# Spectral layer and MLP on one core: transform steps at the end of a tick, a first stage over 128 partitions, two tables at other addresses

## The chip, the core and the metric

One core of a Trainium2 chip runs the whole program. The metric is the device time of one launch in microseconds (us), median of three runs. Engines: PE multiplies matrices, PEld is its weight load, ACT (ScalarE), DVE (VectorE) and POOL (GpSimd) work element by element, SP only issues DMAs. PE writes PSUM; ACT and DVE read it; POOL does not.

## The reference

`x` is 4 batches of 3008 x 256 floats. Per batch: a real FFT along the 3008 positions, a complex 256 x 256 product with bias, a soft threshold, the inverse FFT; then an MLP over all 12032 tokens.

```python
X = np.fft.rfft(x, axis=1)
Yr = Xr @ w_r - Xi @ w_i + b_r
Yi = Xr @ w_i + Xi @ w_r + b_i
Yr = np.sign(Yr) * np.maximum(np.abs(Yr) - 0.01, 0.0)      # Yi likewise
y = np.fft.irfft(Yr + 1j * Yi, n=3008, axis=1)
h = y.reshape(12032, 256) @ w_in                            # 256 -> 2048
out = (h / (1 + np.exp(-h))) @ w_out                        # 2048 -> 256
```

## The kernel before

**The transform** is split as 3008 = 47 x 64 and done with tables of sines and cosines as matrix products. The first stage (47 points) goes to DRAM scratch `scr1`; second stage, complex product, threshold and third stage run over 12 steps `u` per batch (2 of 24 residues each) and go to `scr2`; the last stage `i2` reads `scr2` and leaves 512 tokens at a time in `xt`, in the MLP's layout. Precision is kept by splitting each operand in a high and a low part (`fp32r`) and adding three products.

**The MLP** goes in *ticks*: one tick is one block of 512 tokens and 128 of the 2048 hidden channels. `mlp1` (L631, 12 matmuls) writes one of two PSUM banks tagged `h`; ACT applies Silu (L638) and casts the high part `gh` (L647), DVE forms the low part `gl` (L648); `mlp2` (L789, 12 matmuls) adds into the `acc` banks. The `gh`, `gl` of tick t are made at the head of tick t+1 and are used by `mlp2` in tick t+2.

**The order.** `manual_schedule` means that each engine works in the order in which the code issues. A dictionary `fill` holds the transform's work by tick: what is put at an integer t stands between `mlp1` and `mlp2` of that tick, what is put at t + 0.5 stands behind `mlp2`, at the tick's end. A planner fills ticks 24 to 146 for batches 1 to 3 with three kinds of work:

- a *piece* (`stack_split`, `stack_product`, L294 to L317): one sixteenth of the first stage of batch 2 or 3. The 47 rows stand at partitions 0 to 46, and their low parts at 64 to 110, so one product over 111 partitions does both. Its four matmuls (L308) write two banks, which ACT (L312) and DVE (L313) read;
- a *step* (`u3_step` with half 0): the second stage `s2_3` (L417, 8 passes) into one bank, read by ACT L425, L426 and DVE L429; then the split of an earlier threshold result (ACT L474, DVE L475), and the third stage `i1` (L489, 6 matmuls) into another bank, read by ACT L493. A step also issues the loads `a`, `t2` (SP) and `t3` (POOL);
- a *mix* (`u3_step` with half 1): `mix3`, 18 matmuls (L442) into two banks. The first is copied by ACT L448, POOL adds the biases (L449, L450); the second is read by four DVE instructions (L461) of `shrink`, which is deferred to the head of the next tick, ahead of its `gl`.

All of these share two PSUM banks, `d0` and `d1`, one after the other (`bank`, L182). A piece that follows a step therefore writes the bank that `s2_3` wrote and then the bank that `i1` wrote; a piece that follows a mix writes the mix's two banks in turn. Each must wait until the readers are done.

`shift(pool, n)` allocates n bytes that nobody uses, to move what follows it in SBUF. Later there are *fast* ticks (blocks 10 to 22, L717), in which only `i2` is left of the transform.

Of the kernel before, what the change touches and what calls it, by code (L numbers as in the profile page):

```python
# [18 lines left out]
S, D, DFF, NB = 3008, 256, 2048, 4  # L19
RR, KK = 47, 64  # L20
# [129 lines left out]
def spectral_mlp_kernel(ctx: ExitStack, tc: tile.TileContext, x, w_r, w_i, b_r, b_i, w_in, w_out, c1, c2, c3, c4, c3f, c5, out):  # L150
    nc = tc.nc
    cst = ctx.enter_context(tc.tile_pool(name="cst", bufs=1))
    sb = ctx.enter_context(tc.tile_pool(name="sb", bufs=2))
    tf = tc.alloc_tile_pool(name="tf", bufs=1)
# [3 lines left out]
    def shift(pool, n):  # L158

        state["shifts"] += 1  # L160
        pool.tile([128, n // 4], F32, bufs=1, name=f"shift{state['shifts']}")
# [20 lines left out]
    def bank(name):  # L182

        state["d"] += 1
        tag, bufs = f"d{state['d'] % 2}", 1
        if state["prologue"]:
            k = state["d"] % 8
            tag, bufs = (("d0", 1), ("acc", 3), ("h", 2), ("acc", 3), ("d1", 1), ("acc", 3), ("h", 2), ("e0", 1))[k]
        if state["fast"]:
            tag = "d1"  # L190
        return ps.tile([128, 512], F32, tag=tag, bufs=bufs, name=name)
# [3 lines left out]
    def store(dst, src, late=False):  # L195

        if late or not state["prologue"]:
            stores.append((dst, src))
        else:
            nc.scalar.dma_start(out=dst, in_=src)  # L200

    def flush(n):
        for dst, src in stores[:n]:
            nc.sync.dma_start(out=dst, in_=src)
        del stores[:n]
# [17 lines left out]
    def x_load_twice(b, q):  # L223

        t = x_sb[q % 2]
        if b == STACKED and q < 2:
            nc.gpsimd.memset(t[32:64, :], 0.0)
        h, g = divmod(q, 8)
        v = x[b].rearrange("(n h j) d -> n h (j d)", h=2, j=NJ)[:, h, g * 4 * D:(g + 1) * 4 * D]
        for p in (0, 64):  # L230
            nc.gpsimd.dma_start(out=t[p:p + RR, :], in_=v)
        return t
# [3 lines left out]
    def x_ahead():  # L236
        if x_next:
            q = x_next.pop(0)
            x_t[q] = (x_load_twice if q[0] >= STACKED else x_load)(*q)
# [8 lines left out]
    def s1(b, g, late=False):  # L248
        for _ in s1_halves(b, g, late):
            pass  # L250
# [43 lines left out]
    def stack_split(b, q):  # L294
        t = x_t[b, q]
        sx = tf.tile([128, 4 * D], F32R, tag="sx", bufs=1, name="sx")
        nc.scalar.copy(sx[:64 + RR, :], t[:64 + RR, :])
        nc.vector.tensor_sub(sx[64:64 + RR, :], t[64:64 + RR, :], sx[64:64 + RR, :])
        x_t[b, q] = sx

    def stack_product(b, q):
        sx = x_t.pop((b, q))
        o = tf.tile([128, 4 * D], F32, tag="s1o", bufs=2, name="s1o")[:2 * NR, :]
        for i in range(2):
            p = bank("s1")
            c = slice(i * 512, (i + 1) * 512)
            for k in range(2):
                nc.tensor.matmul(  # L308
                    out=p[:, k * D:(k + 1) * D], lhsT=c5_sb[:64 + RR, :],
                    rhs=sx[:64 + RR, (2 * i + k) * D:(2 * i + k + 1) * D], start=True, stop=True,  # L310
                )
            nc.scalar.copy(o[:, c], p[64:64 + 2 * NR, :])  # L312
            nc.vector.tensor_tensor(out=o[:, c], in0=p[:2 * NR, :], in1=o[:, c], op=ALU.add)  # L313
        h, g = divmod(q, 8)
        v = scr1[b].rearrange("r (i h j) d -> (r i) h (j d)", i=2, h=2)
        store(v[:, h, g * 4 * D:(g + 1) * 4 * D], o)
        x_ahead()  # L317
# [15 lines left out]
    def t2_load(b, u):  # L333
        t2 = tf.tile([128, 256], F32, tag="t2", bufs=3, name="t2")
        nc.sync.dma_start(out=t2, in_=c2[:, u * 256:(u + 1) * 256])
        t2_t[b, u] = t2
# [141 lines left out]
    def i1(b, u):  # L478
        z = u_t.pop((b, u))
        t3 = t3_t.pop((b, u))  # L480
        p = bank("i1")
        pv = p.rearrange("p (a c) -> p a c", a=2)
        for r in range(2):
            q = slice(r * 128, (r + 1) * 128)
            if b == 0:
                nc.tensor.matmul(out=pv[:, r, :], lhsT=t3[:, q], rhs=z[:, r, :], start=True, stop=True)  # L486
                continue
            for n, (m, k) in enumerate(((0, 0), (0, 1), (1, 0))):
                nc.tensor.matmul(  # L489
                    out=pv[:, r, :], lhsT=t3[:, m, q], rhs=z[k][:, r, :], start=(n == 0), stop=(n == 2),  # L490
                )
        o = tf.tile([128, 2, D], F32, tag="i1o", bufs=2, name="i1o")
        nc.scalar.copy(o, pv)  # L493
        store(scr2[b][2 * u:2 * u + 2].rearrange("r p d -> p r d"), o)
# [331 lines left out]
    def w_split(t, dst, eng):  # L826
        nc.scalar.copy(dst[0], t)
        eng.tensor_sub(dst[1], t, dst[0])
# [43 lines left out]
    with tc.manual_schedule():  # L872
# [6 lines left out]
        c5_sb = tf.tile([128, 128], F32R, name="c5_sb")  # L879
# [35 lines left out]
        def w_ahead():  # L915
            if weights:
                src, *rest = weights.pop(0)
                w_loaded.append((w64_load(src), *rest))
# [3 lines left out]
        def w_begin():  # L922

            w_ahead()
            if w_loaded:
                w_run.append([0, w64_split(*w_loaded.pop(0))])
                next(w_run[-1][1])
# [27 lines left out]
        def u_step(u):  # L955
            if u < NU:
                if u + 3 < NU:
                    u_load(0, u + 3)
                t3_load(0, u)
                s2(0, u)  # L960
            if u > 2:
                w_go()
            if 0 <= u - 1 < NU:
                mix(0, u - 1)
            if u % 2 and 2 < u < NU:
                w_go()
            if 0 <= u - 2 < NU:
                i1(0, u - 2)

        t2_load(0, 0)  # L970
        for g in range(8):
            s1(0, g)
            if g < 3:
                x_ahead()
# [8 lines left out]
        warm(zero, 5)  # L983
        w_split(w32[0], wr, nc.vector)
        w_split(w32[1], wi, nc.gpsimd)
        for u in range(NU):
            u_step(u)
            if u == 0:
                w_ahead()
            if u == 2:  # L990
                w_begin()
            if u in (3, 4):
                flush(1)
            if u in (2, 3, 5, 7, 9):
                x_ahead()
            if u == 8:
                nc.sync.dma_start(out=c4_sb, in_=c4)
# [16 lines left out]
        g_load(0, 1, cols=slice(2 * D, 4 * D))  # L1014
        s1(1, 4, late=True)
        w_go()
        shift(tf, 192)
        w_tags[:] = [(("zl", 2), ("zh", 2))]
        s1(1, 5, late=True)
        flush(2)  # L1020
# [17 lines left out]
        def at(t, fn, *args):  # L1038
            fill.setdefault(t, []).append((fn, args))
# [33 lines left out]
        steps = []  # L1073
# [12 lines left out]
        done, t, since = 37, 24, 0  # L1086
        while steps or turned:
            boundary = t % NFF == 1 and t > 32
            stage = None
            if not boundary and t not in taken:  # L1090
                b = steps[0][0] if steps else NB
                ready = b in stacked and t >= stacked[b] + (4 if b > 1 else 0)
                apart = 2 + (ready and b > 1 and len(pieces_left) % 2)
                if pieces_left and t >= done + apart and pieces_left[0][0] <= b + 1:
                    stage = "piece"
                elif ready:
                    stage = "mix" if steps[0][2] else "step"
            more = None
            if turned and t >= turned[0][0] and t >= since + 2 and not (boundary and t < turned[0][1]):
                if stage in ("mix", None) or t >= turned[0][1]:  # L1100
                    more = turned.pop(0)[2]
                    since = t
            if stage == "piece":
                at(max(t - 2, done), stack_split, *pieces_left[0])
                at(t, stack_product, *pieces_left[0])
                done = t
                if pieces_left.pop(0)[1] == 15:
                    stacked[max(stacked) + 1] = t
            elif stage:
                if b not in begun:  # L1110
                    begun.add(b)
                    for k in range(2):
                        at(t - 2 + k, u_load, b, k)
                at(t, u3_step, *steps.pop(0))
                last = t
                ended[b] = t
            if more:
                at(t + 0.5 * (stage is not None), *more)
                if more[0] is i2_ends:
                    at(t - 2, i2_load, more[1], True)  # L1120
            t += 1
# [3 lines left out]
        for i in range(FAST[0], len(BLOCKS)):  # L1125
            if i in FAST:
                first = max(16 * i - 13, last + 1)
                t = last_stage(i, first)
# [14 lines left out]
        for q in range(NFF // 2):  # L1143
            steps = fast_weights(q)
# [20 lines left out]
        for t in range(len(ticks) + 1):  # L1165
            i, f = ticks[t] if t < len(ticks) else (LAST, None)
# [68 lines left out]
```

## Time and profile before

| | |
|---|---|
| median of three runs | 1302.69 us (1302.64 to 1303.19) |
| the profiled execution | 1301.09 us |
| its span, first to last instruction | 1298.7 us |
| PE busy in the span | 1285.1 us, 99% |
| ACT, DVE, POOL busy | 790.6, 890.1, 200.3 us |
| TensorE clock granted | 0.998 of full speed |

PE is busy all but 13.6 us of the span, and 92% of the chain that ended last is PE. The matmuls overlap, so that their durations (some 277 ns each) say little; the distance from one start to the next is what a matmul costs, and the chain of waits gives it for a group in one number (1.36 us for 12 matmuls, for example).

### The profile page before, as it was taken

The page shows a single profiled execution, that of the slowest core. Times are in us where ns is not written, and L with a number is a line of the kernel's source. Part 1 is how long each engine was busy: PE and PEld are TensorE (multiplying, and loading weights), DVE is VectorE, ACT ScalarE, POOL GpSimd, SP SyncE. Part 2 cuts the span into 40 slices and gives each one's busy share as a digit, 9 for nine tenths or more (in the row PEclk, how much of TensorE's full clock was granted, in tenths as well). Part 3 has the DMA queues.
Part 4 walks back from the last instruction along what each step waited for, and adds up shares of the span by engine and source line. Part 5 has one row for each costly group of instructions (what it writes and reads, how often), then busy time and mean ns, then how long its engine had stood idle before and what let it go on. Part 6 is the DMA issues. An engine that isn't in the chain of part 4 may idle for free.

```text
span 1298.7 us, 27507 instructions
## 1 busy us (share of the span) xinstructions
PE 1285.1 (99%) x10933; PEld 1259.9 (97%) x10933; DVE 890.1 (69%) x1697; ACT 790.6 (61%) x1640; POOL 200.3 (15%) x296
## 2 busy tenths in 40 slices
PE   8999999999999999999999999999999999999998
PEld 3988999999999999999999999999999999999998
DVE  3777757778767777566658666667666666766663
ACT  5456655767666656555555666566656665666655
POOL 2000002222212221111202111210112101110200
PEclk9999999999999999999999999999999999999999
DMA  8886414554465543423220110011001110110000
GB/s 267 265 239 197 140 52 121 132 150 108 118 161 153 119 130 102 129 82 119 84 75 2 48 33 12 22 33 32 14 11 48 33 32 2 33 33 14 5 24 25
DMA packets 76166, 110.29 MB, mean 85 GB/s; under 512 B 8880, under 2 KB 54824, under 8 KB 76040
## 3 DMA queue, kind: packets, MB, share of 16 engines
q1 hardware_dynamic: 61921, 79.17, 20.8%
q0 software_dynamic: 10544, 25.68, 8.0%
q10 hardware_dynamic: 3575, 3.70, 0.9%
q8 instruction: 86, 1.41, 0.5%
q14 instruction: 40, 0.33, 0.1%
HBM read 71.03 MB, written 37.49 MB: 84 GB/s over the span
## 4 chain that ended last, share of the span: by engine, by line
PE 92%; DMA 4%; ACT 2%; DVE 1%; issue 0%; POOL 0%; SPq 0%; ACTq 0%; DVEq 0%
PE acc L789 38%; PE h L717 19%; PE h L631 16%; PE mix L442 5%; PE s L417 3%; PE i L489 2%; PE mix L382 2%; PE i L558 2%; PE i2e L558 1%; PE s L308 1%; DMA scr<-s1o 1%; PE s L269 1%; DMA t3f<-in_c3f_dram 1%; PE s L351 1%; PE i L486 1%; DMA out_dram<-o 1%
## 5 line engine op out<-in xcount | busy, mean ns | idle before, releaser
L789 PE MATMUL acc<-wout,gh 128*128 128x256 f32 x3008 | 541.4, 277 | 0.0
L789 PEld LDWEIGHTS acc<-wout,gh 128*128 128x128 f32 x3008 | 454.6, 188 | 1.1 <-issue 0.5
L789 PE MATMUL acc<-wout,gl 128*128 128x256 f32 x1504 | 416.3, 277 | 1.4 <-DVE gl L648 1.4
L789 PEld LDWEIGHTS acc<-wout,gl 128*128 128x128 f32 x1504 | 282.3, 188 | 1.8 <-DVE gl L648 1.8
L631 PE MATMUL h<-xt,win 128*128 128x256 f32 x2016 | 259.6, 277 | 0.4 <-ACT xt L590 0.3
L631 PEld LDWEIGHTS h<-xt,win 128*128 128x128 f32 x2016 | 242.6, 188 | 0.8 <-ACT xt L590 0.5
L638 ACT ACTIVATE g<-h 128x512 f32<-128x512 f32 (+1 forms) x177 | 101.9, 576 | 148.2 <-PE h L631 146.6
L765 DVE TENSOR_TENSOR gl<-gp,gh 128x512 fp32r<-128x512 f32 x208 | 145.7, 701 | 25.1 <-ACT gh L764 24.4
L755 ACT ACTIVATE gp<-gp 128x256 f32<-128x256 f32 x104 | 43.5, 418 | 180.1 <-DVE gp L752 180.1
L648 DVE TENSOR_TENSOR gl<-g,gh 128x512 fp32r<-128x512 f32 (+1 forms) x177 | 117.4, 664 | 46.9 <-ACT gh L647 45.4
L764 ACT CAST gh<-gp 128x512 fp32r<-128x512 f32 x208 | 129.5, 622 | 6.5
L647 ACT CAST gh<-g 128x512 fp32r<-128x512 f32 (+1 forms) x177 | 106.2, 600 | 1.1 <-PE acc L789 0.2
L717 PE MATMUL h<-xt,win 128*128 128x256 f32 x624 | 106.2, 279 | 0.0
L757 DVE TENSOR_TENSOR gp<-h,u 128x256 f32<-128x256 f32 x104 | 44.1, 424 | 78.7 <-ACT gp L756 78.7
L461 DVE TENSOR_TENSOR y<-q,mix 64x256 f32<-64x256 f32 x144 | 60.3, 419 | 41.9 <-PE mix L442 35.0
L717 PE MATMUL h<-th,sw_h 128*128 128x256 f32 x312 | 87.4, 280 | 0.0
L717 PEld LDWEIGHTS h<-xt,win 128*128 128x128 f32 x624 | 86.4, 188 | 0.1
L717 PE MATMUL h<-th,sw_l 128*128 128x256 f32 x312 | 86.2, 276 | 0.0
L717 PE MATMUL h<-tl,sw_h 128*128 128x256 f32 x312 | 86.2, 276 | 0.0
L449 POOL TENSOR_TENSOR q<-q,bias 128x256 f32<-128x256 f32 x36 | 28.9, 804 | 340.6 <-ACT q L448 340.6
L752 DVE TENSOR_TENSOR gp<-h,u 128x256 f32<-128x256 f32 x104 | 44.2, 425 | 50.7 <-PE h L717 49.2
L763 ACT ACTIVATE gp<-gp 128x512 f32<-128x512 f32 x104 | 66.3, 638 | 0.0
(169 smaller groups left out, 2325.3 us busy)
## 6 DMA issues: line engine op xcount, KB each, us to landing
a<-scr SPq DMA_DIRECT2D x48, 256.0 KB
x_sb<-in_x_dram POOLq DMA_DIRECT2D x64, 188.0 KB, 3.9
gin<-scr SPq DMA_DIRECT2D x48, 192.0 KB
t<-in_c_dram POOLq DMA_DIRECT2D x36, 256.0 KB, 3.7
scr<-i1o SPq DMA_DIRECT2D x36, 256.0 KB
t<-in_c_dram SPq DMA_DIRECT2D x48, 128.0 KB
scr<-s1o SPq DMA_DIRECT2D x32, 192.0 KB
scr<-s1o SPq DMA_DIRECT2D x13, 384.0 KB
```

What stands on the lines that cost most here:

```text
L442: nc.tensor.matmul(out=out, lhsT=x_[:, e, c, :], rhs=m[:, e, :], start=(n == 0), stop=(n == 5))
L461: nc.vector.tensor_tensor(out=y[64 * i:64 * i + 64, r, :], in0=q[rows, i, :], in1=pv[rows, i, :], op=op,)
L631: nc.tensor.matmul(out=p[:, c:c + D], lhsT=w[:, e, f * 128:(f + 1) * 128], rhs=v[:, e, c:c + D], start=(m == 0), stop=(m == 5),)
L638: nc.scalar.activation(out=g[:, q], in_=p[:, q], func=ACTF.Silu)
L647: nc.scalar.copy(gh[:, q], g[:, q])
L648: nc.vector.tensor_sub(gl[:, q], g[:, q], gh[:, q])
L717: nc.tensor.matmul(out=p, lhsT=w[j], rhs=m[k], start=(begins and n == 0), stop=(n == 2), skip_group_check=True,)
L752: nc.vector.tensor_tensor(out=g[:, 1, :], in0=px[:, 0:HB], in1=u, op=ALU.add)
L763: nc.scalar.activation(out=v, in_=v, func=ACTF.Silu)
L764: nc.scalar.copy(h, v)
L765: nc.vector.tensor_sub(l, v, h)
L789: nc.tensor.matmul(out=a[:, r, :], lhsT=v[:, q], rhs=wout[:, f, w, :], start=(begins and m == 0 and r == 0), stop=(ends and m == 2), skip_ ...
```

## The change

Three edits, all in the transform:

- The piece's product runs over all 128 partitions: ACT casts 128 instead of 111, DVE subtracts on 64 instead of 47, the rows between are set to zero by one more memset on POOL for each of the two buffers.
- Steps and mixes go from t to t + 0.5, behind the tick's `mlp2`. Pieces stay where they are, between `mlp1` and `mlp2`. Work of the last stage (`i2`, `i2_ends`) that shares a tick with a step or a mix goes the other way, from behind `mlp2` to ahead of it.
- Three `shift` calls are added, one gets another size. In the built program the second-stage tables `t2` go from 0 to 192 modulo 256 bytes, the third-stage tables `t3f`, `t3` and the tiles `y`, `i1o` from 0 to 128; `a`, `xh`, `xl` (0) and `zh`, `zl` (192) stay.

In the changed kernel the lines from L228 on are one further (L309 for L308), near the end up to four.

```diff
         if b == STACKED and q < 2:
-            nc.gpsimd.memset(t[32:64, :], 0.0)
+            for p in (32, 96):
+                nc.gpsimd.memset(t[p:p + 32, :], 0.0)
...
-        nc.scalar.copy(sx[:64 + RR, :], t[:64 + RR, :])
-        nc.vector.tensor_sub(sx[64:64 + RR, :], t[64:64 + RR, :], sx[64:64 + RR, :])
+        nc.scalar.copy(sx, t)
+        nc.vector.tensor_sub(sx[64:128, :], t[64:128, :], sx[64:128, :])
...
-                    out=p[:, k * D:(k + 1) * D], lhsT=c5_sb[:64 + RR, :],
-                    rhs=sx[:64 + RR, (2 * i + k) * D:(2 * i + k + 1) * D], start=True, stop=True,
+                    out=p[:, k * D:(k + 1) * D], lhsT=c5_sb,
+                    rhs=sx[:, (2 * i + k) * D:(2 * i + k + 1) * D], start=True, stop=True,
...
+        shift(tf, 192)
         t2_load(0, 0)
+        shift(tf, 64)
...
         w_split(w32[1], wi, nc.gpsimd)
+        shift(tf, 128)
         for u in range(NU):
...
-        shift(tf, 192)
+        shift(tf, 64)
         w_tags[:] = [(("zl", 2), ("zh", 2))]
...
-                at(t, u3_step, *steps.pop(0))
+                at(t + 0.5, u3_step, *steps.pop(0))
...
             if more:
-                at(t + 0.5 * (stage is not None), *more)
+                at(t + 0.5 * (stage == "piece"), *more)
```

PE around a step that a piece follows, before: the `s2_3` rows write the tile `s_3651`, `i1` writes `i_3669`, the piece writes `s_3711` and `s_3716`.

```order
L631 MATMUL h<-xt_2693,win_82 128x256
L417 MATMUL s_3651<-t_3135,a 128x2x64 x4
L489 MATMUL i_3669<-zh,t_2916 128x256
...
L789 MATMUL acc<-wout,gh 128x256 x2
...
L631 MATMUL h<-xt_2692,win_82 128x256
...
L308 MATMUL s_3711<-sx,c_sb 128x256 x2
L308 MATMUL s_3716<-sx,c_sb 128x256 x2
```

The same place after the change, with the tiles under new numbers and the lines one further:

```order
L632 MATMUL h<-xt_2653,win_82 128x256
L790 MATMUL acc<-wout,gh 128x256 x2
...
L418 MATMUL s_3668<-t_3152,a 128x2x64 x4
L490 MATMUL i_3686<-zh,t_2933 128x256
...
L632 MATMUL h<-xt_2652,win_82 128x256
...
L309 MATMUL s_3715<-sx,c_sb 128x256 x2
L309 MATMUL s_3720<-sx,c_sb 128x256 x2
```

Between the end of `i1` and the piece there stood `mlp2` and `mlp1`, 24 matmuls; now there stands `mlp1` alone, 12.

PE from a mix to the piece behind it, before:

```order
L442 MATMUL mix<-ws_80,xl 128x256
L789 MATMUL acc<-wout,gh 128x256 x2
...
L631 MATMUL h<-xt_2692,win_82 128x256
...
L308 MATMUL s_3595<-sx,c_sb 128x256 x2
L308 MATMUL s_3600<-sx,c_sb 128x256 x2
```

And after, where this tick's part of the last stage (L559) has gone ahead of `mlp2`:

```order
L559 MATMUL i_3524<-c_sb,gin 128x141 x2
L790 MATMUL acc<-wout,gh 128x256 x2
...
L443 MATMUL mix<-ws_80,xl 128x256
L632 MATMUL h<-xt_2652,win_82 128x256
...
L309 MATMUL s_3600<-sx,c_sb 128x256 x2
L309 MATMUL s_3605<-sx,c_sb 128x256 x2
```

Here too `mlp2` has gone from behind the mix to ahead of it, and only `mlp1` is left between the mix and the piece.

## Rows read from the trace of the kernel before

**Rows 1.** Page: the span, PE's busy time, the last chain by engine.
```profile
span 1298.7 us, 27507 instructions
PE 1285.1 (99%) x10933; PEld 1259.9 (97%) x10933; DVE 890.1 (69%) x1697; ACT 790.6 (61%) x1640; POOL 200.3 (15%) x296
PE 92%; DMA 4%; ACT 2%; DVE 1%; issue 0%; POOL 0%; SPq 0%; ACTq 0%; DVEq 0%
```
**Rows 2.** Groups by shape, PE: count | busy us, mean ns | idle before.
```profile
L417 PE MATMUL s<-t,a 128*128 128x128 f32 x288 | 38.1, 275 | 0.7 <-DVE s1o L313 0.7
L442 PE MATMUL mix<-wr,xh 128*128 128x256 f32 x144 | 26.3, 276 | 0.0
L308 PE MATMUL s<-sx,c_sb 111*128 111x256 f32 x128 | 20.4, 282 | 0.0
```
**Rows 3.** Timeline of PE, 317 to 335 us: start, duration, what.
```profile
320.59 1.05 PE L417 MATMUL s<-t,a 128*128 128x128 f32 x8
321.39 0.36 PE L489 MATMUL i<-zh,t 128*128 128x256 f32 x1
...
322.19 0.40 PE L789 MATMUL acc<-wout,gh 128*128 128x256 f32 x2
...
324.96 0.64 PE L308 MATMUL s<-sx,c_sb 111*128 111x256 f32 x4
...
330.25 0.39 PE L789 MATMUL acc<-wout,gh 128*128 128x256 f32 x2
```
**Rows 4.** Timeline of ACT, 317 to 335 us.
```profile
321.67 0.59 ACT L425 CAST xh<-s 128x512 fp32r<-128x512 f32 x1 [0.29 <-PE s L417]
322.16 0.38 ACT L426 COPY xs<-s 128x256 f32<-128x256 f32 x1
323.02 0.41 ACT L428 CAST xh<-xs 128x256 fp32r<-128x256 f32 x1 [0.49 <-DVE xs L427]
323.34 0.62 ACT L474 CAST zh<-y 128x512 fp32r<-128x512 f32 x1
323.86 0.58 ACT L493 COPY i1o<-i 128x512 f32<-128x512 f32 x1
...
326.74 1.05 ACT L297 CAST sx<-x_sb 111x1024 fp32r<-111x1024 f32 x1
```
**Rows 5.** Timeline of DVE, 317 to 335 us.
```profile
322.91 0.68 DVE L429 TENSOR_TENSOR xl<-s,xh 128x512 fp32r<-128x512 f32 x1
...
330.52 1.72 DVE L461 TENSOR_TENSOR y<-q,mix 64x256 f32<-64x256 f32 x4 [0.75 <-PE mix L442]
...
333.34 0.69 DVE L648 TENSOR_TENSOR gl<-g,gh 128x512 fp32r<-128x512 f32 x1
```
**Rows 6.** Chain that ended last, 325 to 372 us: start, us, what.
```profile
325.12 0.47 PE s L308 x4
325.59 1.42 PE acc L789 x12
327.01 1.36 PE h L631 x12
...
354.17 1.42 PE h L631 x12
...
369.78 1.41 PE acc L789 x12
```
**Rows 7.** Timeline of PE, 236 to 239 us.
```profile
237.59 1.16 PE L417 MATMUL s<-t,a 128*128 128x128 f32 x8 [0.39 <-DVE s1o L313]
238.50 0.36 PE L489 MATMUL i<-zh,t 128*128 128x256 f32 x1
```
**Rows 8.** Timeline of POOL, 100 to 260 us.
```profile
211.79 0.94 POOL L227 MEMSET x_sb<- 32x1024 f32 x1
...
219.31 0.73 POOL L449 TENSOR_TENSOR q<-q,bias 128x256 f32<-128x256 f32 x1 [4.67 <-ACT q L448]
```
**Rows 9.** Chain that ended last, 715 to 732 us.
```profile
725.02 3.95 DMA gin<-scr
```

## The prediction, made before the changed kernel was run

> **What bounds the kernel now.** I read the page first: PE is busy 1285.1 of 1298.7 us and holds 92% of the last chain [rows 1]. So the end comes later by whatever keeps PE waiting, and earlier by whatever makes its matmuls follow closer. Next the groups by shape: the reader is to see that PE hardly waits for the transform today, 0.7 us in all in front of the second stage (L417), nothing in front of the pieces (L308) or the mixes (L442) [rows 2]. Then the chain, which gives groups of 12 matmuls from start to start: 1.36 us where PE runs evenly, 1.42 us behind a piece and 1.41 us behind a step [rows 6]. Last the timelines of PE, ACT and DVE through one step, one piece and one mix [rows 3 to 5]: they tell how long after PE's last write the two shared PSUM banks are read out.
>
> **Steps at the end of a tick: the term that decides.** A piece must wait for the readers of both banks. The order shows that between a step or a mix and the piece of the next tick one group of 12 goes away: 24 matmuls stood there (2.72 us), now 12 (1.36 us). Counted in the order of the changed kernel, 10 pieces follow directly on a full step, 14 on a mix, 1 on a step that has only the second stage; the other 7 of the 32 follow on neither, or on a third stage alone, whose one copy is short, and I count no wait for them.
>
> *Step, then piece.* The second stage ends at 321.39, where L489 starts, and `i1` at 322.19: 0.80 us [rows 3]. ACT reads the first bank (L425, L426), makes a sum and a split (L428, L474), and only then copies `i1`'s bank: L493 from 323.86 for 0.58, to 324.44, 3.05 us after the second stage [rows 4]. `i1` itself is long done; what is late is ACT's chain, and it starts only when PE delivers, so that an idle ACT doesn't shorten it. After the change PE reaches the piece's second half at 0.80 + 1.36 + 0.24 (half of 0.47 [rows 6]) = 2.40 us. It waits 0.65 us. (The first half needs L429, which ends at 323.59 [rows 5], 2.20 us after; due at 2.16, so this wait lies within the other.) Before, the piece was due 1.36 us later, at 3.76, which is why no wait shows.
>
> *Mix, then piece.* The mix ends at 330.25 [rows 3]. The four L461 that read its second bank run from 330.52 for 1.72, to 332.24, 1.99 us after [rows 5]. PE is there at 1.36 + 0.24 = 1.60: it waits 0.39 us.
>
> *Second stage alone, then piece.* Its only bank is the piece's second; L429's end at 2.20 against 1.60: 0.60 us.
>
> Each wait also costs a restart. One that the trace has in front of a step, at 237.59, shows it: the eight passes of L417 last 1.16 us there and 1.05 without a wait [rows 3, 7], so 0.11. Sum: 10 x 0.76 + 14 x 0.50 + 0.71 = 15.3 us. What queues behind a waiting piece on PE is its tick's `mlp2`, and with it everything: no later slack takes these waits back, since PE has none. The price from below is zero, if the readers were early; from above I add 0.05 per wait for the way from a reader's end to PE, 1.3 in all, an estimate.
>
> *What goes away.* From a piece to the next step or mix there are now 36 matmuls, not 24, so the waits of L417 on DVE L313 go: 0.7 us idle [rows 2] and two restarts, 0.9 us. Nothing else becomes late there: the piece's readers need less than the 2.7 us at which they were just too slow.
>
> *Behind the steps.* `mlp2` no longer follows a step: 36 x 0.05 (1.41 less 1.36) saves 1.8. `mlp1` does now; the row of 354.17, where it follows other transform matmuls, gives 1.42 [rows 6], so up to 36 x 0.06 = 2.2 is paid. I take 0, between -1.8 and 2.2. The 14 parts of the last stage that go ahead of `mlp2` trade one follower for another too: 14 x 0.06 either way, taken as 0.
>
> *DMAs that move.* A step's loads of `a` and `t2` (SP) and `t3` (POOL) leave half a tick later and serve a step at least two ticks on: 0. The stores of `i1` are queued at the end of a tick and leave with the next one. In the order the last `i1` of batch 1 stands five ticks ahead of the part of the last stage that reads it, so one tick less is covered; were it not, each of three batches could pay one load of 3.95 us [rows 9].
>
> **The first stage over 128 partitions.** The four matmuls of a piece take 0.47 us where four of the 128-row kind take 4/12 of 1.36 = 0.45, and their mean is 282 ns beside 276 for L442 of the same size [rows 2, 6]. And `mlp2` behind them takes 1.42, not 1.36. I put both on the 111 rows, as the piece is the one group of this size without 128: 32 x (0.02 + 0.06) = 2.6 us saved. From below 0, if it is something else.
> The Trainium skill speaks against this term: by TensorE: Matmul & The Clock Gate, section LDWEIGHTS (loading the stationary operand), a weight load takes as long over 32 rows as over 128, and only the columns count. By it the 2.6 us would stay, and the sum would be that much higher. The trace rather disagrees, with 282 against 276 ns, but has no matmul at both sizes.
> Around the matmuls: ACT's cast L297 takes 1.05 us [rows 4]; ACT's time goes by columns, not partitions, so 0, and were it by partitions 0.16 more, in ticks where ACT waits for PE anyway (it is busy 61%, [rows 1]). The two more memsets take 0.94 us each on POOL, which idles 4.67 us next to the one shown [rows 8]: 0, at most 1.9 if a load of `x` came late by it.
>
> **The tables' addresses.** No row shows the same matmul at two addresses. The nearest difference of pace between matmuls of one size is 1.42 against 1.36 per 12, 5 ns each; over the 648 matmuls and passes of second and third stage that is 3.2 us either way. I take 0, since nothing says which way.
>
> **Sum.** 15.3 - 0.9 - 2.6 = 11.8 us. The profiled execution took 1301.1 (its span 1298.7 and 2.4 around it): 1312.9. The median of the runs is 1.6 higher, 1302.7, and it is a median that is to be predicted: 1314.5 us. Its own range is 1309 to 1320 by the bounds named.
>
> **Rivals.**
> 1. *The 111 rows cost nothing.* Same waits, no gain from the full rows: 1314.5 + 2.6 = 1317. For it speaks that `mlp2` behind a step is just as slow with 128 rows (1.41); against it that the piece's own four are slow from the first. Chance 0.12. This is what the Trainium skill's page TensorE: Matmul & The Clock Gate would have.
> 2. *Not slower: the banks are free in time.* If the readers needed no more than 1.6 us after a mix and 2.4 after a step, no piece would wait. What is left are the gains, 2.6 + 0.9, with the upper bound of the addresses 3.2 and of the followers 1.8: 1294 to 1299, say 1298. For it: DVE and ACT have one group more to catch up before a step or mix. Against it: the chains of [rows 4, 5] begin with idle time ended by PE (0.29 and 0.75), so they are at their shortest. It decides from 0.65 and 0.39 us of shortening on. Chance 0.08.
> 3. *No change.* The mixes' waits vanish (14 x 0.50 = 7.0) and the addresses give their 3.2: 11.8 - 10.2 = 1.6, so 1304. Needs two of the above at once. Chance 0.07.
> 4. *DVE comes late as well.* `shrink` now stands at the head of the next tick with its mix just done, and `gl` behind it ends 3.78 us after the mix (334.03) [rows 5]. `mlp2` wants it at the third matmul two ticks on, 3 x 1.36 + 0.23 = 4.31 us where no piece lies between. If DVE ran more than 0.53 us late, each of 36 mixes might pay some 0.3: 11 more, 1325. Chance 0.05.
>
> **Chances.** The forecast itself has 0.68. A difference under 0.2% (2.6 us) can't be told from none here. Slower by more: 0.68 + 0.12 + 0.05 = 0.85; within: 0.07; faster: 0.08. Range 1305 to 1320: the forecast's own and rival 1, and downward part of the way to rival 3.
>
> **What would show it.** In the changed kernel's groups, L309 (the piece) should have some 12 us idle before it, ended by DVE L462 and ACT L494, in 25 places; L418's 0.7 should be gone. L309's mean should be 276 ns and `mlp2` behind a piece without a wait 1.36 us. Without idle time before L309 the forecast is wrong in its main term; with it and a time under 1309, the tables or the followers gave more than their bounds.

## The result, and the profile after

| | before | after |
|---|---|---|
| median | 1302.66 us (1300.04 to 1303.19, 4 runs) | 1314.37 us (1313.06 to 1316.73, 4 runs) |
| profiled execution, its span | 1301.09, 1298.7 | 1313.06, 1311.2 |
| ratio | | 1.0091, interval 1.007 to 1.0111 |

The change makes the kernel slower, by 11.7 us; the forecast was 1314.5. The same two programs on another chip gave 1317.71 (1315.99 to 1320.04, 6 runs) against 1301.81 (1299.0 to 1309.45, 23 runs), ratio 1.0103 (1.0078 to 1.0127). By how much single executions of one program differ, and where, is part of what follows.

The page of the changed kernel, against [rows 1]: the span grows by 12.5 us, PE's busy time by 5.5 only, and PE's share of the last chain falls from 92 to 89%.

```profile
span 1311.2 us, 27504 instructions
PE 1290.6 (98%) x10933; PEld 1258.9 (96%) x10933; DVE 888.6 (68%) x1697; ACT 788.1 (60%) x1640; POOL 201.8 (15%) x298
PE 89%; DVE 4%; DMA 3%; ACT 3%; issue 1%; POOL 0%; SPq 0%; DVEq 0%; ACTq 0%
```

The groups of PE that answer to [rows 2] (count, busy us and mean ns, idle time before and what ended it), then PE's waits (us in total, times, longest) and those of its weight load, PEld, for `gl`, after and before:

```profile
L418 PE MATMUL s<-t,a 128*128 128x128 f32 x288 | 37.9, 274 | 0.0
L309 PE MATMUL s<-sx,c_sb 128*128 128x256 f32 x128 | 27.1, 302 | 9.0 <-DVE y L462 5.6 <-ACT i1o L494 2.8 <-DVE xl L430 0.4
L443 PE MATMUL mix<-wr,xh 128*128 128x256 f32 x144 | 26.3, 276 | 0.0
```
```profile
PE s L309 <- DVE y L462: 5.6, 14, 0.7
PE s L309 <- ACT i1o L494: 2.8, 10, 0.3
PEld acc L790 <- DVE gl L649: 2.2, 4, 1.4
PE s L309 <- DVE xl L430: 0.4, 1, 0.4
```
```profile
PEld acc L789 <- DVE gl L648: 1.8, 2, 1.4
```

The pieces now wait, in 14, 10 and 1 places, for the three readers that the prediction named, and the wait in front of the second stage is gone. `mlp2` waits for `gl` in four places instead of two: the two new ones stand behind a piece, at 406.36 and 543.91, where `mlp2` takes 1.75 and 1.62 us instead of 1.36. The chain through one step, its piece, one mix and its piece (start, us, what) shows each wait whole:

```profile
308.10 0.91 PE s L418 x8
...
310.69 0.44 ACT zh L475
...
311.21 0.59 ACT i1o L494
311.80 0.04 issue
311.84 0.50 PE s L309 x2
...
316.49 2.05 PE mix L443 x18
...
319.93 0.43 DVE y L462
320.36 0.14 issue
320.50 0.47 PE s L309 x2
320.98 1.41 PE acc L790 x12
```

Between the step and the piece, and between the mix and the piece, the chain runs over ACT and over DVE; in [rows 6] it ran over PE alone. A piece that follows neither is 20 us later in the same view: 0.45 us for four matmuls and 1.36 for the `mlp2` behind.

```profile
343.48 0.45 PE s L309 x4
343.93 1.36 PE acc L790 x12
```

PE's timeline of the same places, the answer to [rows 3]; the rows give what a piece costs from start to start:

```profile
308.74 0.36 PE L490 MATMUL i<-zh,t 128*128 128x256 f32 x1
...
309.53 1.54 PE L632 MATMUL h<-xt,win 128*128 128x256 f32 x12
311.08 0.47 PE L309 MATMUL s<-sx,c_sb 128*128 128x256 f32 x2
311.84 0.50 PE L309 MATMUL s<-sx,c_sb 128*128 128x256 f32 x2 [0.28 <-ACT i1o L494]
312.18 0.40 PE L790 MATMUL acc<-wout,gh 128*128 128x256 f32 x2
```
```profile
318.37 1.52 PE L632 MATMUL h<-xt,win 128*128 128x256 f32 x12
319.73 0.39 PE L309 MATMUL s<-sx,c_sb 128*128 128x256 f32 x2
320.50 0.47 PE L309 MATMUL s<-sx,c_sb 128*128 128x256 f32 x2 [0.38 <-DVE y L462]
320.81 0.40 PE L790 MATMUL acc<-wout,gh 128*128 128x256 f32 x2
```

Behind the step the piece takes 1.10 us (311.08 to 312.18), and `mlp1` before it 1.55 instead of 1.36; behind the mix it takes 1.08. The idle time in brackets is less than what is lost (0.28 and 0.38 against some 0.64), because PE's modelled ends overlap the wait: the starts are to be read, not the brackets.

ACT's timeline, against [rows 4]: `i1`'s copy ends at 311.79, 3.05 us after the second stage (308.74), as in the kernel before; the cast of a piece (L298) takes 1.05 us over 128 partitions as it did over 111 [rows 4].

```profile
311.21 0.58 ACT L494 COPY i1o<-i 128x512 f32<-128x512 f32 x1
```

**Where the time went.** One stretch holds every step, mix and piece of batches 1 to 3: from the first `mlp1` of tick 20 to the first L718 (L717 before) that uses `sw_h`. In PE's timeline it runs from the first of these rows to the second, in the kernel before and in the changed one:

```profile
158.69 0.50 PE L631 MATMUL h<-xt,win 128*128 128x256 f32 x3
...
712.09 0.28 PE L717 MATMUL h<-th,sw_h 128*128 128x256 f32 x1
```
```profile
155.59 0.62 PE L632 MATMUL h<-xt,win 128*128 128x256 f32 x4
...
724.55 0.28 PE L718 MATMUL h<-th,sw_h 128*128 128x256 f32 x1
```

That is 569.0 us, against 553.4 before: 15.6 more. In the repeat on another chip it is 569.6 (160.63 to 730.18), 16.2 more. Outside the stretch PE's order is the same, but single executions differ there: the profiled one of the changed kernel reached tick 20 at 155.6, the repeat at 160.6, before at 158.7. Two executions of one kernel agree in the stretch within 0.6 us (three kernels have two: this one, the one before and the one with the rows alone). So it is the better ruler for a difference of 2 us, and each experiment below is read by it beside its median.

### The profile page after: what moved, and what is told of

Read it like the earlier page. It is cut to its first block, busy times and chain, and to the rows that moved or that the text cites. A ratio compares the mean times of both kernels' runs of the same rounds, so it can differ in the third digit from the quotient of the medians.

```text
span 1311.2 us, 27504 instructions
## 1 busy us (share of the span) xinstructions
PE 1290.6 (98%) x10933; PEld 1258.9 (96%) x10933; DVE 888.6 (68%) x1697; ACT 788.1 (60%) x1640; POOL 201.8 (15%) x298
## 3 DMA queue, kind: packets, MB, share of 16 engines
q8 instruction: 86, 1.41, 0.4%
## 4 chain that ended last, share of the span: by engine, by line
PE 89%; DVE 4%; DMA 3%; ACT 3%; issue 1%; POOL 0%; SPq 0%; DVEq 0%; ACTq 0%
PE acc L790 38%; PE h L718 18%; PE h L632 14%; PE mix L443 5%; PE mix L383 3%; PE s L418 2%; DVE y L462 2%; PE i2e L559 2%; PE i L559 2%; PE i L490 1%; PE s L309 1%; DMA scr<-s1o 1%; PE s L270 1%; PE i L487 1%; PE s L352 1%
## 5 line engine op out<-in xcount | busy, mean ns | idle before, releaser
L718 PE MATMUL h<-xt,win 128*128 128x256 f32 x624 | 106.2, 279 | 0.0
L462 DVE TENSOR_TENSOR y<-q,mix 64x256 f32<-64x256 f32 x144 | 60.3, 419 | 66.7 <-PE mix L443 61.7
L718 PE MATMUL h<-th,sw_h 128*128 128x256 f32 x312 | 87.5, 280 | 0.0
L718 PEld LDWEIGHTS h<-xt,win 128*128 128x128 f32 x624 | 86.4, 188 | 0.1
L718 PE MATMUL h<-th,sw_l 128*128 128x256 f32 x312 | 86.3, 277 | 0.0
L718 PE MATMUL h<-tl,sw_h 128*128 128x256 f32 x312 | 86.2, 276 | 0.0
```

The lines of the kernel that those rows point to most:

```text
L462: nc.vector.tensor_tensor(out=y[64 * i:64 * i + 64, r, :], in0=q[rows, i, :], in1=pv[rows, i, :], op=op,)
L718: nc.tensor.matmul(out=p, lhsT=w[j], rhs=m[k], start=(begins and n == 0), stop=(n == 2), skip_group_check=True,)
```

## The experiments

Theory throughout: the loss is the pieces' wait for the two banks, as there is only one group of 12 matmuls left to cover the readers. Ratios are against the kernel before on the same chip: 1302.74 us (29 runs) for the first four experiments, 1301.81 (23 runs) for the next three.

**Steps and mixes back at t, the other two edits kept.**

```diff
-                at(t + 0.5, u3_step, *steps.pop(0))
+                at(t, u3_step, *steps.pop(0))
...
-                at(t + 0.5 * (stage == "piece"), *more)
+                at(t + 0.5 * (stage is not None), *more)
```

> The changed kernel with the steps, the mixes and the parts of the last stage put back to their places of before; the 128 rows and the new addresses stay. Theory W (25 pieces wait for the readers of the two shared banks, because 12 matmuls instead of 24 lie between): no idle time before the piece, L418's 0.7 us of waiting for DVE is back, all 32 pieces run their four matmuls in 0.45 us and leave mlp2 at 1.36, and the time is 1296 to 1300 us. Rival (the rows or the addresses make it slower, the moved steps do not): the time stays above 1310 and the slow places are found without any moved step.

Measured: 1301.39 us (1297.23 to 1304.69, 12 runs), ratio 0.9983 (0.9967 to 0.9999); stretch 551.4 (161.20 to 712.63). The groups of this kernel:

```profile
L418 PE MATMUL s<-t,a 128*128 128x128 f32 x288 | 38.1, 275 | 0.9 <-DVE s1o L314 0.9
L309 PE MATMUL s<-sx,c_sb 128*128 128x256 f32 x128 | 19.7, 276 | 0.0
```

The 9.0 us idle before L309 are gone and the old wait of the second stage is back. The move alone is worth 569.0 - 551.4 = 17.6 us; the other two edits together give back 2.0. The median is 1.4 above the expected range.

**Pieces moved along, behind `mlp2` as well**, so that 24 matmuls stand between them and the step or mix ahead.

```diff
-                at(max(t - 2, done), stack_split, *pieces_left[0])
-                at(t, stack_product, *pieces_left[0])
+                at(max(t - 2, done + 0.5), stack_split, *pieces_left[0])
+                at(t + 0.5, stack_product, *pieces_left[0])
...
-                at(t + 0.5 * (stage == "piece"), *more)
+                at(t, *more)
```

> The changed kernel with the pieces moved to the end of their tick as well, so that 24 matmuls lie again between a step or mix and the piece behind it, while steps and mixes stay behind mlp2. Theory W: the waits before L309 go, 1296 to 1300 us. Rival (work at a tick's end is late for its own users, DVE above all, whose shrink then stands ahead of gl): still 1308 or more, with idle time before mlp2 ended by DVE gl.

Measured: 1302.64 us (1299.58 to 1306.81, 11 runs), ratio 1.0003 (0.9985 to 1.002); stretch 551.7 (160.53 to 712.18), as short as with nothing moved. Of the pieces' waits one is left; `mlp2` waits for `gl` more often:

```profile
L309 PE MATMUL s<-sx,c_sb 128*128 128x256 f32 x128 | 20.0, 277 | 0.5 <-DVE y L462 0.5
```
```profile
PE acc L790 <- DVE gl L649: 2.4, 4, 1.2
```

The median missed its range by 2.6 us. 24 of the 25 waits go although the steps and mixes stay at the tick's end: the distance to the piece decides. This is the strongest of the tests, for it keeps the moved steps and takes the cause away. But the move is not free by itself. Two of the four waits for `gl` lie in the stretch and are new: there `mlp2` takes 2.22 us (at 400.18) and 2.10 (at 530.49) instead of 1.36, 1.6 us together, and the piece that still waits loses 0.7. That is the rival's mechanism, in two places and far from the 1308 us that it needed. It is made up for by the two waits of the second stage and one of `i1`, which are gone here and cost 1.7 us from start to start with nothing moved.

**Only the mixes at the end of the tick.**

```diff
-                at(t + 0.5, u3_step, *steps.pop(0))
+                at(t + 0.5 * (stage == "mix"), u3_step, *steps.pop(0))
...
-                at(t + 0.5 * (stage == "piece"), *more)
+                at(t + 0.5 * (stage in ("piece", "step")), *more)
```

> The changed kernel with only the mixes at the end of a tick and the steps back between mlp1 and mlp2. Theory W: 14 pieces wait, each costs 0.65 us by the trace of the changed kernel (the piece takes 1.09 us from its start to mlp2 there, 0.45 without a wait), 9 us in all above the kernel with nothing moved: 1305 to 1308. Rival (only the sum of both moves makes ACT and DVE late): no waits, 1297 to 1300.

Measured: 1307.54 us (1305.01 to 1311.93, 12 runs), ratio 1.0043 (1.003 to 1.0057); stretch 560.3 (159.96 to 720.24), 8.9 more than with nothing moved. The pieces wait in fourteen places, all for L462:

```profile
PE s L309 <- DVE y L462: 5.8, 14, 0.9
```

**Only the steps at the end of the tick.**

```diff
-                at(t + 0.5, u3_step, *steps.pop(0))
+                at(t + 0.5 * (stage == "step"), u3_step, *steps.pop(0))
...
-                at(t + 0.5 * (stage == "piece"), *more)
+                at(t + 0.5 * (stage in ("piece", "mix")), *more)
```

> The changed kernel with only the steps at the end of a tick and the mixes back between mlp1 and mlp2. Theory W: 11 pieces wait (10 for ACT's copy of i1, 1 for DVE), each costs 0.65 us in the piece and up to 0.18 in the mlp1 before it, 7 to 9 us above the kernel with nothing moved: 1304 to 1307. Rival (only the sum of both moves makes ACT and DVE late): no waits, 1297 to 1300.

Measured: 1312.9 us (1311.67 to 1313.61, 4 runs), ratio 1.0078 (1.0056 to 1.0099); stretch 565.0 (159.11 to 724.15), 13.6 more than with nothing moved. The expectation is missed by 6 us. The ten waits of the pieces are there; what I left out are the mixes (the waits of their weight load; "issue" names no releaser):

```profile
PEld s L309 <- ACT i1o L494: 4.9, 10, 0.5
PEld mix L443 <- issue: 3.0, 17, 0.2
```

A step at the end of a tick and a mix in the middle of the next have only 12 matmuls between them too, and share the same two banks. A mix without a wait takes 2.04 us. Of the 17, 13 follow a full step: they take 2.24, with 1.56 for the `mlp1` ahead of them. Four follow a second stage alone; in the chain one of these takes 2.34:

```profile
394.36 0.89 PE s L418 x8
395.25 1.42 PE h L632 x12
396.67 2.34 PE mix L443 x18
```

Read off the starts in PE's timeline, the 17 mixes and the `mlp1` ahead of them lose 6.4 us together, about the miss. That they wait for the banks' readers shows in the starts, though no view names it: the first matmul of the 13 begins 0.15 us after the end of L430, which reads the first bank. With both kinds moved a mix follows a step by 24 again and waits nowhere (L443 above: 0.0 idle). So the two halves of the move don't add up to the whole: 8.9 + 13.6 is more than 17.6.

**In a step, `i1` ahead of the split**, so that ACT copies `i1`'s bank before it casts `zh`.

```diff
-                if 0 <= u - 2 < NU:
-                    split_z(b, u - 2)
                 if 0 <= u - 3 < NU:
                     i1(b, u - 3)
+                if 0 <= u - 2 < NU:
+                    split_z(b, u - 2)
```

> The changed kernel with i1 issued ahead of split_z in a step, so that ACT copies i1's bank (L494) before it casts zh (L475), 0.52 us earlier. Theory (the piece behind a step waits for ACT's chain): the wait for L494 falls from about 0.45 to under 0.1 us in the 10 places, the first half's 0.18 stays: 4 us less than the changed kernel, 1310.3, with the 14 waits behind mixes as they were. Rival (what is late is not the order on ACT but the way from reader to PE or the restart): no change, 1314.4.

> The changed kernel unaltered, so that the next ones are compared with it on the same chip. 1313 to 1315.5 us; 25 pieces wait, 10 on ACT L494 and 14 on DVE L462 and one on DVE L430, some 9 us idle before L309.

Measured: 1312.64 us (1310.36 to 1319.98, 6 runs) against 1317.71 for the changed kernel on the same chip: 5.1 less, where 4 was expected. Both medians came out above what was expected of them, by 2.3 and 2.2. The stretch is 564.0 (159.54 to 723.52) against 569.6. ACT and PE behind one step, in this kernel:

```profile
313.22 0.58 ACT L494 COPY i1o<-i 128x512 f32<-128x512 f32 x1
313.69 0.62 ACT L475 CAST zh<-y 128x512 fp32r<-128x512 f32 x1
```
```profile
312.06 1.54 PE L632 MATMUL h<-xt,win 128*128 128x256 f32 x12
313.62 0.74 PE L309 MATMUL s<-sx,c_sb 128*128 128x256 f32 x4
314.19 0.40 PE L790 MATMUL acc<-wout,gh 128*128 128x256 f32 x2
```

The copy ends at 313.80, the four matmuls of the piece go as one group and take 0.57 us instead of 1.10. Over the ten places that is 5.2 us, nearly all of the 5.6 in the stretch; the 14 waits for L462 stay (5.6 us idle). The wait hangs on the order on ACT, not on the way from ACT to PE.

**The rows alone, and the addresses alone**, each put into the kernel before.

```diff
-                    out=p[:, k * D:(k + 1) * D], lhsT=c5_sb[:64 + RR, :],
+                    out=p[:, k * D:(k + 1) * D], lhsT=c5_sb,
...
```

The other lines of the first are those of the change for the 128 partitions; the second has the four `shift` lines of the change.

> The kernel before with the 128-row piece alone. Theory (the 111 rows cost 0.02 us in the piece and 0.06 in the 12 matmuls behind it): 32 x 0.08 = 2.6 us less than before, 1300.1, L309 at 0.45 us per four and 1.36 us for the twelve mlp2 behind it. Rival (only columns count, the two addresses gave what was seen with the steps back at t): 1302.7, four in 0.47 and twelve in 1.42 as before.

> The kernel before with the four shifts alone, 111 rows as before. Theory: the addresses are worth nothing, 1302.7, the stretch from the first batch's end to the fast ticks within 0.3 us of before (599.8). Rival: they give the 2 us that the rows don't, 1300.7, with a shorter L418 or L490 from start to start.

Measured: the rows alone 1300.58 us (1297.68 to 1306.6, 12 runs), ratio 0.998 (0.9961 to 1.0), stretch 551.1 (160.85 to 711.96); the addresses alone 1304.22 (1299.08 to 1307.74, 12 runs), ratio 1.0006 (0.9986 to 1.0025), stretch 553.9 (157.29 to 711.16). In the chains a piece and the `mlp2` behind it, first over 128 rows, then with the addresses changed and 111 rows:

```profile
252.34 0.45 PE s L309 x4
252.79 1.36 PE acc L790 x12
```
```profile
248.90 0.47 PE s L308 x4
249.37 1.42 PE acc L789 x12
```

All 32 pieces of the first are like this, and 31 of the second. The rows give 2.3 us in the stretch, the addresses nothing that can be told (0.5 more). In the longer stretch that was expected within 0.3 us of 599.8 they took 600.3, a miss of 0.2; the kernel before took 600.0 there in its second execution.

**One program, two executions.** Two single executions, of the kernel before and of the one with the rows alone, were to tell whether the last 580 us belong to the program or to the execution.

> The kernel before, unaltered, one execution. Theory (the pace of 1.36 or 1.41 us per 12 matmuls in the last 580 us is a matter of the single execution): the time falls anywhere between 1298 and 1309, and if it is above 1304 the part from the first L717 with sw_h on, which no edit touches, is longer than 582.4 us by that much, with mlp2 at 1.41 there. Rival (that part's pace belongs to the program, and the runs scatter in the first 100 us alone): 582.4 us again, whatever the time.

> The kernel with the 128-row piece alone once more, one execution. Theory (pace by execution): the part from the first L718 with sw_h on differs from the 587.3 us of the first execution, most likely 582 to 584. Rival (pace by program): 587.3 again, with mlp2 at 1.41 from 20 us after its start on. In both: 0.45 us for the piece's four, 1.36 for the twelve behind them, and 2.0 to 2.5 us less than before (553.4) from tick 20 to there.

Measured: 1300.82 and 1302.04 us. From the first `sw_h` to the last matmul the kernel with the rows took 587.3 us in its first execution (1306.55 us in all) and 583.8 in the second; before took 582.4 and 582.6. The granted clock was 1.00 both times in the stretch from 732 to 872 us, and yet PE started 1192 matmuls in it the first time and 1222 the second (the columns are us, busy time of each engine with its count, clock, DMA share, GB/s):

```profile
732.00:872.00 140.00, 140.00 (x1192) 140.00 (x1192) 93.54 (x193) 84.11 (x188) 20.65 (x26) 1.00 0.08 23
```
```profile
732.00:872.00 140.00, 140.00 (x1222) 140.00 (x1221) 94.34 (x196) 85.90 (x193) 22.62 (x29) 1.00 0.08 23
```

So one program shows both paces. The two executions ran on different chips, which alone does not rule the chip out; but on the chip of the first, twelve runs of this program spread from 1297.68 to 1306.6 us, so the single execution matters. The expectation for the kernel before was not put to the test: its second execution took 1300.82 us, and the signs that it named were for one above 1304. In the stretch with the transform the pace did not spoil the comparison: 553.4 and 553.6 for before, 551.1 and 551.3 for the rows.

## Why the prediction was right, point by point

- **Places: right.** 25 waits, 14 for L462, 10 for L494, 1 for L430, none of a piece elsewhere. Of the signs that were named, L309's idle time came out lower (9.0 us for some 12) and its mean higher (302 ns for 276): a wait goes in part into the modelled durations.
- **Sizes: each a little low.** An undisturbed piece takes 0.453 us and the groups beside it 1.360. Over the 14 places behind a mix the piece takes 1.105 on average and `mlp2` 1.400: 0.69 lost, forecast 0.50. Over the 10 behind a step the piece takes 1.095, `mlp1` before it 1.556, `mlp2` 1.391: 0.87 lost, forecast 0.76. The single second stage loses 0.76 (the `mlp1` behind it takes 1.50 with or without a wait), forecast 0.71. In sum 9.7 + 8.7 + 0.8 = 19.2 us, forecast 15.3. The readers ended when I said they would (L494 3.05 us after the second stage, L462 1.99 after the mix: 318.37 to 320.36). Behind the mix the missing part is the way to PE, 0.14 us from L462's end to the piece's start; I had allowed 0.05 and put it in the bound alone. Behind the step the second half starts 3.10 us after the second stage (308.74 to 311.84) where it was due at 2.38, so 0.72 late where I had 0.65, and restart and slower followers take 0.15 where I had 0.11; the first half's wait does lie within the second's.
- **What goes away: right, but too small.** L418 has no idle time; it is back with the steps at t (0.9). The 0.9 us were read from idle times; from start to start the two waits cost 0.66 and 0.63 us in the kernel before (`mlp1` ahead of L417 takes 1.91 and 1.88 us), and a third, of `i1` behind a mix at 504.31, 0.30. All three are gone: 1.6 us.
- **What the sum put at nothing: `gl`.** The two new waits of `mlp2` cost 0.4 and 0.3 us, 0.7 together.
- **The rows: right, -2.3 where I had -2.6.** The rows-only kernel has the same matmuls at both sizes, which the trace of before lacked: 0.475 against 0.453 us for a piece, 1.418 against 1.360 for the twelve behind it. Rival 1 would have kept 0.475 and 1.418, and is out; by its time alone (1317) the repeat would have spoken for it. The Trainium skill (TensorE: Matmul & The Clock Gate, section LDWEIGHTS) says that the number of rows loaded doesn't matter to a weight load; the trace does show 188 ns for the loads at both sizes, yet the matmuls keep another distance. In the changed kernel most of the second part of this gain is lost again: behind a piece that waited, `mlp2` mostly runs at 1.41 with 128 rows too.
- **Followers and addresses: near 0, as taken.** 19.2 + 0.7 - 1.6 - 2.3 = 16.0, against 15.6 and 16.2 in the stretch. The parts of the last stage that changed places were not moved alone.
- **Rivals 2, 3 and 4.** All 14 mixes' waits are there, so 2 and 3 are out. Rival 4's mechanism is there, but in two places and 0.7 us, not in 36 and 11 us.
- **The median was hit more closely than the sum deserves.** The sum said 11.8, the stretch shows 15.6 to 16.2: that the median came within 0.2 us of the forecast is luck. Of the first four runs the profiled one was short elsewhere, for it reached tick 20 3.1 us ahead of the kernel before; the others have no trace. The repeat is 15.9 us above the kernel before on its chip, which is what the corrected sum gives, and at 1317.7 still within the range.

No version here beats the kernel before by much. Both with the 128-row piece and nothing moved come out 0.2% below it, with intervals that end at 0.9999 and 1.0; in the stretch they are 2.0 and 2.3 us shorter.

## What to carry to other kernels

Where two PSUM banks are passed from one kind of work to the next, count the matmuls between the last write and the next one, and compare their time with the end of the readers' chain, not with the one reader that is written down: behind a step it was ACT's order (`zh` ahead of the copy), not `i1`, that set the wait. When a kind of work is moved, do that for every pair of neighbours on both sides of it, and do it again for each half of the move. Read the waits of the weight load too: the two new ones for `gl` show there, while PE's own idle time hides them. On an engine that is 99% busy, measure such a change in the stretch that it touches, from start to start, since the rest of the run scatters by more than the effect.

## What the runs showed that I had not expected

- **PE keeps one of two distances between matmuls of this size, 113.3 or 117.8 ns (1.36 or 1.41 us per 12), at the same granted clock of 1.00**, and can keep the slower one for well over 100 us. In the part of the run after the first `sw_h` before had 29 matmuls at the slower distance (116 to 119 ns), the first execution of the rows alone 1104; at 4.5 ns each that is 4.8 us, nearly the whole difference between their lengths there (582.4 and 587.3). In the twelve traces this part, in which PE's order is always the same, took 582.4 to 582.6 us five times, 583.8 to 583.9 five times and 587.3 twice. Two rows of the chains at the same place, before and then the rows alone, first execution:

```profile
773.49 1.36 PE acc L789 x12
```
```profile
775.14 1.41 PE acc L790 x12
```

- The 111-row piece put PE into the slower distance for the next twelve matmuls in 32 of 32 places, the 128-row piece in none of 32 in its first execution and in 2 in its second. A wait mostly does. What else sets it was not found.
- From a reader's end to the waiting matmul passed 0.05 us behind ACT's copy in all 10 places and 0.15 behind the last of four DVE instructions in all 14 (0.04 and 0.14 in the chain). It is not the four: behind L430, a single one, it is 0.15 as well, before the first half of the piece in the same 10 places. Why ACT and DVE differ was not tried.
